# Four edits to a fused Fourier layer and two-layer MLP: a later negation, a third transform on 94 columns, operands moved to multiples of 512 bytes, two chunks interleaved

## The chip, the core and the metric

The kernel runs on one core of one Trainium2 chip. The metric is the device time in microseconds of one execution; lower is better. Times are compared as the median of several executions; the profile is one further execution.

## The reference

```python
# x: (2, 3008, 256); w_in: (256, 2048); w_out: (2048, 256); all float32
X = rfft(x, axis=1)
Yr = Xr @ w_r - Xi @ w_i + b_r
Yi = Xr @ w_i + Xi @ w_r + b_i
Y  = softshrink(Yr, 0.01) + 1j * softshrink(Yi, 0.01)
y  = irfft(Y, n=3008)                      # (2, 3008, 256)
x  = y.reshape(6016, 256)
h = x @ w_in1;  x = (max(h, 0) + alpha * min(h, 0)) @ w_out1
h = x @ w_in2;  g = where(h >= 1, h, where(h <= -1, 0, (h + 1)**2 / 4))
out = g @ w_out2
```

## The kernel before

**Fourier part.** The length 3008 is split as 47 x 64, so each transform is two small ones. `f1(g)` (16 groups, 8 per batch) is the first; its results go to DRAM (`store_a`) and come back in another layout (`load_a`). Then come 24 *items* (12 per batch): `f2` is the second transform of an item, and also splits its result into a high part `fh` (ScalarE) and a low part `fl` (VectorE's row `fl<-psf,fh`); `mix` multiplies by the two 256 x 256 weights with 24 matmuls; three VectorE operations add the bias and shrink (`t`, `clip`, `y`); `i1` is the first inverse transform, whose result `ve` goes to DRAM, one store for two items. `p3(g, c)` is the last inverse transform (16 groups, two column halves c, four float32 matmuls each, which the trace shows as eight records); it fills `y`, shown as `yt`. Item loop, step j: `f2` of item j+2, `mix` of j, `i1` of j-2; from j = 16 on also both halves of `p3(j-16)`, one evacuated by ScalarE, one by VectorE. The second batch's `p3` runs inside the MLP, one half per step.

**MLP.** The 6016 rows are 12 *chunks*, six per batch: 512, 512, 512, 512, 512, 448. For each layer l, chunk c and block f of 128 hidden features (16 blocks), `first(l, c, f)` does six matmuls into `psh` and the activation, whose result is split into `gh` and `gl`; `second` does six matmuls into two accumulators `pso`. A float32 product is made of three float32r matmuls, so lines 95, 96 and 97 are low weight by high data, high weight by low data, high by high; the streamed operand has 512 or 448 columns, and the operand loaded ahead of each is 128 x 128. `second` runs three steps behind `first`. `prep(l, c)` splits a chunk's input into `mxh` and `mxl`.

**Split early or late.** For most blocks of layer 0 VectorE makes `gh` at once. Where `late_split` holds (layer 1, and chunk 0 of layer 0) ScalarE makes it, in the step after.

**Weights.** They arrive as 64-bit words and are converted on chip. The generator `conversions` is advanced by `next(conv)`: its first call loads two blocks, then calls alternate between parts 2 and 0 (three operations each on ScalarE and VectorE) and parts 3 and 1 (four on VectorE, then a load of the block after next). Block f is complete after call 2f + 5. In the item loop there are 20 calls (none before j = 4), then one per step of chunk 0. A load is two DMAs of 256 KB from ScalarE's queue.

**Order.** Each engine executes its instructions in program order, and the program order is the order of the Python text. SyncE issues nearly all other DMAs, in text order too:

```python
    load_a(0, A_PARTS[3:])
    for g in range(8, 16):
        f1(g); store_a(g, 0)
    load_mn(1, n_t, c_i1)
    ...
    load_mn(2, m_t, c_f2)          # constants that f2 of items 8 to 11 multiplies by
    load_mn(2, n_t, c_i1)
    nc.sync.dma_start(nalpha, alpha)
    nc.sync.dma_start(g47, c_i2)
    load_a(1, A_PARTS)
```

`m_t[k]` serves `f2` of items 4k to 4k+3. `nalpha` holds alpha; it is negated on VectorE (line 288) and first used by the activation of `first(0, 0, 0)`.

**Addresses.** A tile takes its tag's place, and tags lie one behind another in each partition in the order of their first use. The tags p0 to p5, w0, w1 and m0 to m5 come ahead of `nalpha`, and each starts at a multiple of 512 bytes. `nalpha` takes 64 bytes of a partition, so all tags behind it (the other w and m, the c tags of `mxh` and `mxl`, `gh`, `gl`) start 64 bytes past such a multiple. Weight blocks lie in p, w and m tags (`w_tag`): in layer 0 five of 16 lie at a multiple (f = 10, 11, 13, 14, 15), in layer 1 nine (f = 0 to 5 and 9 to 11).

Of the kernel before, what the change touches and what calls it, by code (L numbers as in the profile page):

```python
# [17 lines left out]
R1, R2 = 47, 64  # L18
# [3 lines left out]
NF = DFF // 128  # L22
# [53 lines left out]
def spectral_mlp_kernel(ctx: ExitStack, tc: tile.TileContext, x, w_r, w_i, bias, c_f1, c_f2,  # L76
                        c_i1, c_i2, w_in1, w_out1, alpha, w_in2, w_out2, out):
    nc = tc.nc
    V, A, G, T = nc.vector, nc.scalar, nc.gpsimd, nc.tensor

    base = ctx.enter_context(tc.tile_pool(name="base", bufs=1))
    rot = ctx.enter_context(tc.tile_pool(name="rot", bufs=2))
    psum = ctx.enter_context(tc.tile_pool(name="psum", bufs=4, space=PSUM))
    dram = ctx.enter_context(tc.tile_pool(name="dram", bufs=1, space=DRAM))

    def split(src, hi, lo, hi_engine):

# [15 lines left out]
    def block(tag, shape, dtype, name):  # L103
        return base.tile(shape, dtype, tag=tag, name=name)
# [16 lines left out]
    def w_of(l, k, f, h, sl):  # L121
        return wt[l, f][:, h, 256 * k + sl * 128:256 * k + sl * 128 + 128]
# [70 lines left out]
    ps = psum.tile([128, 256], F32, tag="h", name="ps_warm")  # L193
# [58 lines left out]
    m_t = [block(f"m{k}", [128, 8, 128], F32, f"m{k}") for k in range(3)]  # L252
    n_t = [block(f"m{3 + k}", [128, 8, 128], F32, f"n{k}") for k in range(3)]
    wm32 = [rot.tile([128, 2, D], F32, tag="tb", name=f"wm32_{k}") for k in range(2)]
    nalpha = base.tile([128, NF], F32, name="nalpha")
    g47 = base.tile([96, 128], F32, name="g47")
    b_t = base.tile([128, 1, D], F32, name="b_t")
    for g in range(8):
# [26 lines left out]
    wm = [block(f"c{k}", [128, 2, 2, D], F32R, f"wm{k}") for k in range(2)]  # L285
    for k in range(2):
        split(wm32[k], wm[k][:, 0], wm[k][:, 1], A)
    V.tensor_scalar(nalpha, nalpha, -1.0, None, op0=ALU.mult)


    items = [(b, i) for b in range(B) for i in range(NK // 2)]
# [51 lines left out]
    for b in range(B):  # L343
        c0 = 0
# [3 lines left out]
    NMAX = max(CHUNKS)  # L348
    NC = len(chunks)
    xc, gt, po = {}, {}, {}  # L350

    def prep(l, c):
        b, c0, n = chunks[c]
        k = 2 * (c % 2)
        xh = block(f"c{k}", [128, 2, NMAX], F32R, f"mxh{l}_{c}")
        xl = block(f"c{k + 1}", [128, 2, NMAX], F32R, f"mxl{l}_{c}")
        split(y[b][:, :, c0:c0 + n], xh[:, :, :n], xl[:, :, :n], A)
        xc[l, c] = xh, xl

    vs, y = {}, [None] * B  # L360

    def load_v(g):
        b, j = divmod(g, 8)
        vs[g] = block(f"m{6 + g % 3}" if b == 0 else f"m{j}", [96, 4, D], F32, f"v{b}_{j}")
        nc.sync.dma_start(vs[g], v_dr[b][:, 4 * j:4 * j + 4, :])

    def p3(g, c, engine):
        b, j = divmod(g, 8)
        if y[b] is None:
            y[b] = block(f"a{b}", [128, 2, S], F32, f"yt{b}")  # L370
        ps = psum.tile([128, 4, 128], F32, tag="h", name=f"ps3_{b}_{j}_{c}")
# [3 lines left out]
        if engine is A:
            A.activation(dst, ps[:, :, 0:94], AF.Copy)
        else:
            V.tensor_copy(dst, ps[:, :, 0:94])


    def late_split(step):
        return step[0] == 1 or step[:2] == (0, 0)

    def split_late(step):
        if step is not None and late_split(step):
            gh, gl, ta = gt[step]
            split(ta, gh, gl, A)

    def first(l, c, f, before):
        n = chunks[c][2]  # L390
        xh, xl = xc[l, c]
        ps = psum.tile([128, NMAX], F32, tag="h", name=f"psh{l}_{c}_{f}")[:, :n]
        for d in range(2):
            mm3(ps, w_of(l, 0, f, 0, d), w_of(l, 0, f, 1, d), xh[:, d, :n], xl[:, d, :n], d == 0, d == 1)
        gh = rot.tile([128, NMAX], F32R, tag="gh", bufs=4, name=f"gh{l}_{c}_{f}")[:, :n]
        gl = rot.tile([128, NMAX], F32R, tag="gl", bufs=4, name=f"gl{l}_{c}_{f}")[:, :n]
        ta = rot.tile([128, NMAX], F32, tag="ta", name=f"ta{l}_{c}_{f}")[:, :n]
        tb = rot.tile([128, NMAX], F32, tag="tb", name=f"tb{l}_{c}_{f}")[:, :n]
        gt[l, c, f] = gh, gl, ta
        if l == 0:  # L400

            A.activation(ta, ps, AF.Relu, scale=-1.0)  # L402
# [33 lines left out]
    conv = conversions(0, list(range(NF)), V, V)  # L436
    n = len(items)
    P3_AT = 16
    for j in range(2):
        f2(*items[j])  # L440
    for j in range(n):
        if j + 2 < n:
            f2(*items[j + 2])
        mix(*items[j])
        if j >= 2:
            i1(*items[j - 2])
        if j == 13:
# [77 lines left out]
```

## Time and profile before

| | us |
|---|---|
| median of 3 runs (lowest, highest) | 1261.45 (1260.71, 1262.11) |
| profiled execution, its own time | 1261.51 |
| its span in the trace | 1259.7 |
| TensorE busy in the span | 1208.5 |
| VectorE / ScalarE busy | 926.3 / 588.7 |

The profiled execution's span is 1.8 us shorter than its own time; its time is within 0.1 us of the median, so differences in the trace can be read as differences in the median. TensorE matmuls overlap in the trace (a record is longer than the distance to the next), so the pace of matmuls is read from their starts.

### The profile page before, as it was taken

What the parts mean: (1) busy time and instruction counts of PE and PEld (TensorE: products, weight loads), DVE (VectorE), ACT (ScalarE), POOL (GpSimd) and SP (SyncE); (2) the same over time, 40 slices, a digit from 0 to 9 for tenths busy, and PEclk for the clock granted to TensorE, in tenths of its full rate; (3) what the DMA queues carried; (4) which work ended last, traced back from release to release, by engine and by line L of the source; (5) the groups of instructions that cost most, each with busy time, mean ns of one, the idle gap of its engine ahead of it and who ended that gap; (6) DMA issues with size and microseconds to landing.
All of it is one profiled execution on the core that took longest, in us unless ns stands there. A gap on an engine that the chain in (4) does not pass through costs nothing.

```text
span 1259.7 us, 15641 instructions
## 1 busy us (share of the span) xinstructions
PE 1208.5 (96%) x5862; PEld 1026.6 (81%) x5862; DVE 926.3 (74%) x1449; ACT 588.7 (47%) x1091; POOL 83.3 (7%) x64
## 2 busy tenths in 40 slices
PE   9179998999999999999999999999999999999998
PEld 6179996878888898888888878888888888888888
DVE  3047787957788999898677798777776777777765
ACT  3035546844555455544444544444444444444443
POOL 0000000000122322131000041000000000000000
PEclk9689998999999999999999999999999999999999
DMA  9943547101010101000000100000000000000000
GB/s 276 290 176 117 158 144 196 39 1 34 18 34 17 34 18 34 17 1 1 1 1 1 51 17 1 18 17 17 1 17 17 15 1 17 18 1 18 17 17 16
DMA packets 37180, 59.30 MB, mean 47 GB/s; under 512 B 3248, under 2 KB 25200, under 8 KB 37104
## 3 DMA queue, kind: packets, MB, share of 16 engines
q1 hardware_dynamic: 23536, 41.37, 10.5%
q10 hardware_dynamic: 13568, 16.93, 4.2%
q8 instruction: 46, 0.75, 0.2%
q14 instruction: 30, 0.25, 0.1%
HBM read 39.55 MB, written 18.74 MB: 46 GB/s over the span
## 4 chain that ended last, share of the span: by engine, by line
PE 90%; DVE 3%; DMA 3%; SPq 2%; ACT 1%; issue 1%; ACTq 0%; DVEq 0%
PE pso L96 13%; PE pso L95 13%; PE psh L95 13%; PE psh L96 13%; PE pso L97 13%; PE psh L97 13%; PE ps L373 2%; PE psm L318 2%; PE psm L320 2%; PE psm L319 2%; PE ps L243 2%; PE psf L298 1%; PE psi L333 1%; SPq L224 1%; DMA a_dr<-ae 1%; DVE gl L92 1%
## 5 line engine op out<-in xcount | busy, mean ns | idle before, releaser
L95 PE MATMUL pso<-gh,w 128*128 128x512 f32 (+1 forms) x768 | 298.6, 389 | 2.8 <-ACT gh L89 2.8
L95 PE MATMUL psh<-mxh,w 128*128 128x512 f32 (+1 forms) x768 | 297.6, 387 | 3.4 <-DVE w L162 2.2
L96 PE MATMUL pso<-gl,w 128*128 128x512 f32 (+1 forms) x768 | 298.3, 388 | 2.5 <-DVE gl L92 2.5
L96 PE MATMUL psh<-mxl,w 128*128 128x512 f32 (+1 forms) x768 | 297.5, 387 | 0.0
L97 PE MATMUL pso<-gh,w 128*128 128x512 f32 (+1 forms) x768 | 296.2, 386 | 0.0
L97 PE MATMUL psh<-mxh,w 128*128 128x512 f32 (+1 forms) x768 | 295.8, 385 | 0.0
L92 DVE TENSOR_TENSOR gl<-ta,gh 128x512 fp32r<-128x512 f32 (+1 forms) x384 | 277.1, 722 | 18.1 <-ACT gh L89 12.0
L410 ACT ACTIVATE ta<-psh 128x512 f32<-128x512 f32 (+1 forms) x192 | 113.1, 589 | 281.6 <-PE psh L97 248.8
L411 DVE SCALAR_TENSOR_TENSOR tb<-ta 128x512 f32<-128x512 f32 (+1 forms) x192 | 131.2, 683 | 137.7 <-ACT ta L410 136.7
L402 ACT ACTIVATE ta<-psh 128x512 f32<-128x512 f32 (+1 forms) x192 | 113.0, 589 | 248.9 <-PE psh L97 215.2
L405 DVE SCALAR_TENSOR_TENSOR ta<-ta,nalpha,tb 128x512 f32<-128x512 f32 (+1 forms) x192 | 166.4, 867 | 64.0 <-ACT tb L403 63.4
L95 PEld LDWEIGHTS psh<-mxh,w 128*128 128x128 f32 x768 | 144.4, 188 | 32.6 <-issue 2.6
L95 PEld LDWEIGHTS pso<-gh,w 128*128 128x128 f32 x768 | 144.5, 188 | 30.9 <-ACT gh L89 3.3
L96 PEld LDWEIGHTS pso<-gl,w 128*128 128x128 f32 x768 | 144.6, 188 | 30.7 <-DVE gl L92 4.7
L97 PEld LDWEIGHTS psh<-mxh,w 128*128 128x128 f32 x768 | 144.4, 188 | 27.9
L97 PEld LDWEIGHTS pso<-gh,w 128*128 128x128 f32 x768 | 144.4, 188 | 27.8
L96 PEld LDWEIGHTS psh<-mxl,w 128*128 128x128 f32 x768 | 144.5, 188 | 26.9
L89 ACT ACTIVATE gh<-ta 128x512 fp32r<-128x512 f32 (+1 forms) x208 | 128.4, 617 | 2.0 <-DVE ta L413 2.0
L413 DVE TENSOR_TENSOR ta<-psh,tb 128x512 f32<-128x512 f32 (+1 forms) x192 | 129.2, 673 | 0.0
L403 ACT ACTIVATE tb<-psh 128x512 f32<-128x512 f32 (+1 forms) x192 | 112.3, 585 | 0.0
L91 DVE CAST gh<-ta 128x512 fp32r<-128x512 f32 (+1 forms) x176 | 79.6, 452 | 18.1
L318 PE MATMUL psm<-wm,fl 128*128 128x256 f32 x192 | 56.3, 293 | 31.2 <-DVE fl L305 31.2
(57 smaller groups left out, 897.5 us busy)
## 6 DMA issues: line engine op xcount, KB each, us to landing
u<-in_w_in ACTq DMA_DIRECT2D x32, 256.0 KB, 2.7
u<-in_w_out ACTq DMA_DIRECT2D x32, 256.0 KB, 3.0
v_dr<-ve SPq DMA_DIRECT2D x12, 512.0 KB, 3.7
v<-v_dr SPq DMA_DIRECT2D x16, 384.0 KB, 6.1
x<-in_x SPq DMA_DIRECT2D x15, 384.0 KB, 8.0
out<-yt SPq DMA_DIRECT2D x20, 256.0 KB, 2.2
a<-a_dr SPq DMA_DIRECT2D x6, 768.0 KB, 6.8
a_dr<-ae SPq DMA_DIRECT2D x20, 192.0 KB, 6.9
```

Of the source, the lines that this page charges most:

```text
L89: A.activation(hi, src, AF.Copy)
L92: V.tensor_tensor(lo, src, hi.bitcast(F32), op=ALU.subtract)
L95: T.matmul(ps, wl, xh, start=start, stop=False)
L96: T.matmul(ps, wh, xl, start=False, stop=False)
L97: T.matmul(ps, wh, xh, start=False, stop=stop)
L318: T.matmul(o, xl[:, j, off:off + 128], wm[r][:, 0, c, :], start=c == r == 0, stop=False)
L402: A.activation(ta, ps, AF.Relu, scale=-1.0)
L403: A.activation(tb, ps, AF.Relu)
L405: V.scalar_tensor_tensor(ta, ta, nalpha[:, f:f + 1], tb, op0=ALU.mult, op1=ALU.add)
L410: A.activation(ta, ps, AF.Relu, bias=0.5, scale=0.5)
L411: V.scalar_tensor_tensor(tb, ta, 1.0, ta, op0=ALU.min, op1=ALU.mult)
L413: V.tensor_tensor(ta, ps, tb, op=ALU.max)
```

## The change

Four edits. (1) The negation of `nalpha` moves from ahead of the item loop into it, at j = 20. (2) `p3` multiplies 94 columns instead of 128 of which 94 were used, and ScalarE evacuates both halves. (3) `nalpha` takes 512 bytes of a partition, so that all tags behind it start at multiples of 512 bytes; for chunks of 448, `mxh`, `mxl`, `gh` and `gl` are used from the 16th column on (`window`), 64 bytes past a multiple. (4) Chunks 0 and 1 of layer 0 go through the blocks together, chunk 1 four blocks behind: blocks 0 to 3 of chunk 0, then 4 of chunk 0, 0 of chunk 1, 5 of chunk 0, 1 of chunk 1, and so on. With it: both chunks split late; `prep(0, 1)` comes at step 2 and `prep(0, 2)` at step 26; the second batch's `p3` starts at step 8 instead of 4; the item loop has one call of the conversions in each step from j = 3 to 21 (19 calls), the MLP's first 32 steps two in every three.

```diff
-    nalpha = base.tile([128, NF], F32, name="nalpha")
+    nalpha = base.tile([128, 128], F32, name="nalpha")[:, 0:NF]
...
-    V.tensor_scalar(nalpha, nalpha, -1.0, None, op0=ALU.mult)
...
+    def window(n):
+        return slice(0, n) if n == NMAX else slice(16, 16 + n)
...
-        split(y[b][:, :, c0:c0 + n], xh[:, :, :n], xl[:, :, :n], A)
+        split(y[b][:, :, c0:c0 + n], xh, xl, A)
...
-    def p3(g, c, engine):
+    def p3(g, c):
-        ps = psum.tile([128, 4, 128], F32, tag="h", name=f"ps3_{b}_{j}_{c}")
+        ps = psum.tile([128, 4, 2 * R1], F32, tag="h", name=f"ps3_{b}_{j}_{c}")
-            T.matmul(ps[:, i, :], vs[g][:, i, c * 128:(c + 1) * 128], g47, start=True, stop=True)
+            T.matmul(ps[:, i, :], vs[g][:, i, c * 128:(c + 1) * 128], g47[:, 0:2 * R1], start=True, stop=True)
+        A.activation(dst, ps, AF.Copy)
...
-        return step[0] == 1 or step[:2] == (0, 0)
+        return step[0] == 1 or step[1] < 2
...
+        if j == 20:
+            V.tensor_scalar(nalpha, nalpha, -1.0, None, op0=ALU.mult)
         if j == n - 2:
             prep(0, 0)
-        for _ in range((j >= 3 and j % 3 != 0) if j < P3_AT else 1 + j % 2):
-            next(conv, None)
+        if 3 <= j < n - 2:
+            next(conv)
...
-    first(0, 0, 1, (0, 0, 0))
-    DEPTH = 3
-    seq = [(l, c, f) for l in range(2) for c in range(NC) for f in range(NF)]
+    DEPTH, LEAD = 3, 4
+    pair = sorted([(0, c, f) for c in range(2) for f in range(NF)], key=lambda s: (s[2] + LEAD * s[1], s[1]))
+    seq = pair + [(l, c, f) for l in range(2) for c in range(NC) for f in range(NF) if (l, c) not in ((0, 0), (0, 1))]
...
-            if 4 <= i < 20:
-                p3(8 + (i - 4) // 2, i % 2, A)
-            if ((l, c) == (0, 0) and f < 15 or (l, c) in ((0, NC - 1), (1, 0)) and f % 2 == 0
+            if i == 2:
+                prep(0, 1)
+            if 8 <= i < 24:
+                p3(8 + (i - 8) // 2, i % 2)
+            if (i < 2 * NF and i % 3 != 0 or (l, c) in ((0, NC - 1), (1, 0)) and f % 2 == 0
                     or l == 0 and c >= 2 and f % 4 == 0):
                 next(conv, None)
```

Three places in the order of instructions. The first is VectorE's queue after the last evacuations of `f1`: the weights' low parts (`wm`), then what stands ahead of the first item's `fl`. Before:

```order
L92 TENSOR_TENSOR wm_321<-wm_0_105,wm_321 128x512
L92 TENSOR_TENSOR wm_322<-wm_1_106,wm_322 128x512
L288 TENSOR_SCALAR nalpha<-nalpha 128x16
L305 TENSOR_TENSOR fl_0_334<-psf_0_328,fh_0_333 128x4x128
L305 TENSOR_TENSOR fl_1_345<-psf_1_339,fh_1_344 128x4x128
```

Of the change:

```order
L92 TENSOR_TENSOR wm_321<-wm_0_105,wm_321 128x512
L92 TENSOR_TENSOR wm_322<-wm_1_106,wm_322 128x512
L304 TENSOR_TENSOR fl_0_333<-psf_0_327,fh_0_332 128x4x128
L304 TENSOR_TENSOR fl_1_344<-psf_1_338,fh_1_343 128x4x128
L304 TENSOR_TENSOR fl_2_355<-psf_2_349,fh_2_354 128x4x128
```

The row on `nalpha` is gone from here; nothing else moved. The second place is ScalarE's queue at steps j = 3 and 4 of the item loop, where `ve` is `i1`'s evacuation, `u` is a raw weight block and `cm` its first conversion. Before:

```order
L336 ACTIVATE ve_0_479<-psi_1_523 128x512
L303 ACTIVATE fh_6_533<-psf_6_528 128x4x128
L304 ACTIVATE fh_6_533<-psf_6_528 128x4x64
L306 ACTIVATE fl_6_534<-fl_6_534 128x4x64
L336 ACTIVATE ve_2_573<-psi_2_570 128x512
L127 DMA u_0_575<-in_w_in 128x2x256
L129 DMA u_0_575<-in_w_out 128x512
L127 DMA u_1_578<-in_w_in 128x2x256
L129 DMA u_1_578<-in_w_out 128x512
```

Of the change:

```order
L335 ACTIVATE ve_0_478<-psi_1_522 128x512
L127 DMA u_0_527<-in_w_in 128x2x256
L129 DMA u_0_527<-in_w_out 128x512
L127 DMA u_1_530<-in_w_in 128x2x256
L129 DMA u_1_530<-in_w_out 128x512
L302 ACTIVATE fh_6_538<-psf_6_533 128x4x128
L303 ACTIVATE fh_6_538<-psf_6_533 128x4x64
L305 ACTIVATE fl_6_539<-fl_6_539 128x4x64
L335 ACTIVATE ve_2_578<-psi_2_575 128x512
L140 ACTIVATE cm_0_580<-u_0_527 128x512
```

The first weight loads stand one item earlier, and the conversion that waits for them follows at the next item. The third place is VectorE's queue at the start of the MLP, where `cm`, `cp`, `w` and `u` are conversions, `ta` is the activation of a block, and `gl_0_0` is what `second(0, 0, 0)` needs. Before:

```order
L326 TENSOR_TENSOR y_1_11_1679<-t_11_1678,clip_11_1677 128x512
L378 COPY yt_1202<-ps_0_7_1_1694 128x376
L161 TENSOR_TENSOR cm_7_1579<-cm_7_1579,w_7_1643 128x512
L162 TENSOR_TENSOR w_7_1643<-cm_7_1579,cp_7_1580 128x512
L168 TENSOR_SCALAR cm_8_1647<-cm_8_1647 128x512
L153 SCALAR_TENSOR_TENSOR cm_8_1647<-cm_8_1647,cp_8_1648 128x512
L158 TENSOR_SCALAR cp_8_1648<-cm_8_1647 128x512
L159 TENSOR_TENSOR cp_8_1648<-cp_8_1648,u_8_1513 128x512
L142 TENSOR_SCALAR cp_9_1712<-u_9_1588 128x512
L405 SCALAR_TENSOR_TENSOR ta_0_0_1730<-ta_0_0_1730,nalpha,tb_0_0_1731 128x512
L92 TENSOR_TENSOR gl_0_0_1729<-ta_0_0_1730,gh_0_0_1728 128x512
```

Of the change:

```order
L325 TENSOR_TENSOR y_1_11_1686<-t_11_1685,clip_11_1684 128x512
L405 SCALAR_TENSOR_TENSOR ta_0_0_1721<-ta_0_0_1721,nalpha,tb_0_0_1722 128x512
L92 TENSOR_TENSOR gl_0_0_1720<-ta_0_0_1721,gh_0_0_1719 128x512
L405 SCALAR_TENSOR_TENSOR ta_0_1_1756<-ta_0_1_1756,nalpha,tb_0_1_1757 128x512
L158 TENSOR_SCALAR cp_8_1537<-cm_8_1536 128x512
L159 TENSOR_TENSOR cp_8_1537<-cp_8_1537,u_8_1329 128x512
L142 TENSOR_SCALAR cp_9_1768<-u_9_1467 128x512
L92 TENSOR_TENSOR gl_0_1_1755<-ta_0_1_1756,gh_0_1_1754 128x512
L405 SCALAR_TENSOR_TENSOR ta_0_2_1781<-ta_0_2_1781,nalpha,tb_0_2_1782 128x512
L92 TENSOR_TENSOR mxl_1_1789<-yt_1240,mxh_1_1788 128x1024
```

Between the last item's `y` and the first block's `ta`, eight rows are gone; `mxl_1`, the second chunk's input, now stands ahead of the third block's `gl`.

## Rows read from the trace of the kernel before

**Rows 1.** The page's part 1: busy us, share of the span, instructions.

```profile
PE 1208.5 (96%) x5862; PEld 1026.6 (81%) x5862; DVE 926.3 (74%) x1449; ACT 588.7 (47%) x1091; POOL 83.3 (7%) x64
```

**Rows 2.** VectorE's timeline, 26 to 90 us: start, duration, operation, [idle before, releaser].

```profile
70.27 0.17 DVE L288 TENSOR_SCALAR nalpha<-nalpha 128x16 f32<-128x16 f32 x1 [33.79 <-DMA nalpha<-in_alpha]
```

**Rows 3.** TensorE's timeline, 38 to 98 us, from the first waiting `mix` on.

```profile
38.81 1.13 PE L298 MATMUL psf<-m,a 128*128 128x128 f32 x8 [1.98 <-DMA m<-in_c_f]
71.09 0.58 PE L318 MATMUL psm<-wm,fl 128*128 128x256 f32 x1 [31.15 <-DVE fl L305]
...
75.69 1.05 PE L298 MATMUL psf<-m,a 128*128 128x128 f32 x8
...
79.41 1.05 PE L298 MATMUL psf<-m,a 128*128 128x128 f32 x8
...
97.44 0.39 PE L298 MATMUL psf<-m,a 128*128 128x128 f32 x2
```

**Rows 4.** SyncE's load of `m_t[2]`: issue time (62 to 75 us) and time to landing.

```profile
L227 SPq DMA_DIRECT2D m<-in_c_f x1: 550/550/550, 63.4 to 63.4; - x1
...
DMA to landing us min/median/max: 5.3/5.3/5.3
```

**Rows 5.** One stretch, all engines: busy us and instructions, granted clock, DMA share, GB/s.

```profile
61.00:66.00 5.00, 0.00 (x0) 0.00 (x0) 0.00 (x0) 0.00 (x0) 0.00 (x0) 0.50 1.03 318
```

**Rows 6.** TensorE's timeline at the start of the MLP, 202 to 254 us.

```profile
202.16 0.50 PE L95 MATMUL pso<-gh,w 128*128 128x512 f32 x1 [2.84 <-ACT gh L89]
...
208.24 2.07 PE L373 MATMUL ps<-g,v 96*128 96x128 f32 x8 [2.59 <-DMA v<-v_dr]
...
209.97 0.77 PE L95 MATMUL pso<-gh,w 128*128 128x512 f32 x1
...
211.82 0.63 PE L96 MATMUL pso<-gl,w 128*128 128x512 f32 x1
212.25 0.63 PE L97 MATMUL pso<-gh,w 128*128 128x512 f32 x1
...
247.74 0.47 PE L95 MATMUL psh<-mxh,w 128*128 128x512 f32 x1 [1.16 <-ACT yt L376]
...
253.86 0.47 PE L95 MATMUL psh<-mxh,w 128*128 128x512 f32 x1 [2.23 <-DVE w L162]
```

**Rows 7.** ScalarE's timeline ahead of the first activation of the MLP.

```profile
196.92 0.63 ACT L156 ACTIVATE w<-cm 128x512 fp32r<-128x512 f32 x1 [4.82 <-DVE cm L153]
...
199.06 0.58 ACT L402 ACTIVATE ta<-psh 128x512 f32<-128x512 f32 x1
```

**Rows 8.** TensorE's timeline: four pairs of starts in the MLP.

```profile
573.45 0.39 PE L95 MATMUL psh<-mxh,w 128*128 128x512 f32 x1
...
589.77 0.39 PE L95 MATMUL psh<-mxh,w 128*128 128x512 f32 x1
...
832.05 0.39 PE L95 MATMUL psh<-mxh,w 128*128 128x512 f32 x1
...
840.29 0.39 PE L95 MATMUL psh<-mxh,w 128*128 128x512 f32 x1
...
446.19 0.37 PE L95 MATMUL psh<-mxh,w 128*128 128x448 f32 x1
...
458.59 0.37 PE L95 MATMUL psh<-mxh,w 128*128 128x448 f32 x1
...
962.81 0.36 PE L95 MATMUL psh<-mxh,w 128*128 128x448 f32 x1
...
970.01 0.36 PE L95 MATMUL psh<-mxh,w 128*128 128x448 f32 x1
```

**Rows 9.** Groups of weight loads by shape: count, busy us, mean ns, idle before.

```profile
L373 PEld LDWEIGHTS ps<-g,v 96*128 96x128 f32 x256 | 33.1, 196 | 4.6 <-DMA v<-v_dr 3.0
...
L243 PEld LDWEIGHTS ps<-x,c 96*96 96x96 f32 x128 | 21.4, 169 | 9.3 <-issue 1.7 <-DMA x<-in_x 0.5
```

**Rows 10.** The chain that ended last, in order of time: start, us, what.

```profile
184.23 1.79 PE ps L373 x16
```

More of the change, by code (lines that the diff above doesn't have):

```diff
@@ L354, in prep @@
         k = 2 * (c % 2)
-        xh = block(f"c{k}", [128, 2, NMAX], F32R, f"mxh{l}_{c}")
-        xl = block(f"c{k + 1}", [128, 2, NMAX], F32R, f"mxl{l}_{c}")
-        split(y[b][:, :, c0:c0 + n], xh[:, :, :n], xl[:, :, :n], A)
+        xh = block(f"c{k}", [128, 2, NMAX], F32R, f"mxh{l}_{c}")[:, :, window(n)]
+        xl = block(f"c{k + 1}", [128, 2, NMAX], F32R, f"mxl{l}_{c}")[:, :, window(n)]
+        split(y[b][:, :, c0:c0 + n], xh, xl, A)
         xc[l, c] = xh, xl
@@ L370, in p3 @@
             y[b] = block(f"a{b}", [128, 2, S], F32, f"yt{b}")
-        ps = psum.tile([128, 4, 128], F32, tag="h", name=f"ps3_{b}_{j}_{c}")
+        ps = psum.tile([128, 4, 2 * R1], F32, tag="h", name=f"ps3_{b}_{j}_{c}")
         for i in range(4):
-            T.matmul(ps[:, i, :], vs[g][:, i, c * 128:(c + 1) * 128], g47, start=True, stop=True)
+            T.matmul(ps[:, i, :], vs[g][:, i, c * 128:(c + 1) * 128], g47[:, 0:2 * R1], start=True, stop=True)
         dst = y[b][:, c, 376 * j:376 * j + 376].rearrange("p (i n) -> p i n", i=4)
[L375 to L378, printed above, removed]
+        A.activation(dst, ps, AF.Copy)
     def late_split(step):
-        return step[0] == 1 or step[:2] == (0, 0)
+        return step[0] == 1 or step[1] < 2
     def split_late(step):
@@ L393, in first @@
         for d in range(2):
-            mm3(ps, w_of(l, 0, f, 0, d), w_of(l, 0, f, 1, d), xh[:, d, :n], xl[:, d, :n], d == 0, d == 1)
-        gh = rot.tile([128, NMAX], F32R, tag="gh", bufs=4, name=f"gh{l}_{c}_{f}")[:, :n]
-        gl = rot.tile([128, NMAX], F32R, tag="gl", bufs=4, name=f"gl{l}_{c}_{f}")[:, :n]
+            mm3(ps, w_of(l, 0, f, 0, d), w_of(l, 0, f, 1, d), xh[:, d, :], xl[:, d, :], d == 0, d == 1)
+        gh = rot.tile([128, NMAX], F32R, tag="gh", bufs=4, name=f"gh{l}_{c}_{f}")[:, window(n)]
+        gl = rot.tile([128, NMAX], F32R, tag="gl", bufs=4, name=f"gl{l}_{c}_{f}")[:, window(n)]
         ta = rot.tile([128, NMAX], F32, tag="ta", name=f"ta{l}_{c}_{f}")[:, :n]
@@ L451, in spectral_mlp_kernel @@
             g = j - P3_AT
-            p3(g, 0, A)
-            p3(g, 1, V)
+            p3(g, 0)
+            p3(g, 1)
             if g + 3 < 8:
                 load_v(g + 3)
+        if j == 20:
+            V.tensor_scalar(nalpha, nalpha, -1.0, None, op0=ALU.mult)
         if j == n - 2:
             prep(0, 0)
-        for _ in range((j >= 3 and j % 3 != 0) if j < P3_AT else 1 + j % 2):
-            next(conv, None)
+        if 3 <= j < n - 2:
+            next(conv)
     i1(*items[n - 2])
@@ L479, in spectral_mlp_kernel @@
                 conv = conversions(1, list(range(12, 16)), V, G)
-            if i >= 2:
+            if i >= 1:
                 first(l, c, f, seq[i - 1])
-            if 4 <= i < 20:
-                p3(8 + (i - 4) // 2, i % 2, A)
-            if ((l, c) == (0, 0) and f < 15 or (l, c) in ((0, NC - 1), (1, 0)) and f % 2 == 0
+            if i == 2:
[3 more added lines that the diff above has]
+            if (i < 2 * NF and i % 3 != 0 or (l, c) in ((0, NC - 1), (1, 0)) and f % 2 == 0
                     or l == 0 and c >= 2 and f % 4 == 0):
                 next(conv, None)
-            if f == NF // 2:
+            if (l, c, f) == (0, 0, NF - 1):
+                prep(0, 2)
+            elif f == NF // 2 and (l, c) not in ((0, 0), (0, 1)):
                 nxt = (l, c + 1) if c + 1 < NC else (l + 1, 0)
```

## The prediction

> **What bounds the kernel now.** I read the page's busy times first. TensorE is busy for 1208.5 of 1259.7 us [rows 1]; no other engine comes near. So a gain must come either from the 51 us in which TensorE waits or from the pace of its matmuls. VectorE's and ScalarE's busy time matters only where TensorE waits for them.
>
> Then I looked for the waits in TensorE's timeline. One is larger than all others together: 31.15 us ahead of the first `mix`, at 71.09 us, for VectorE's `fl` [rows 3]. VectorE's timeline shows why: it stood idle for 33.79 us until alpha had landed, and negated it in 0.17 us at 70.27 [rows 2]; `fl` stands right behind. Sixteen numbers per partition, which no activation needs before 199 us [rows 7], held the queue. The second place is the start of the MLP, where the timeline shows waits of 2.84 and 2.59 us, then steps of 0.43 us at half the clock, then waits of 1.16 and 2.23 us [rows 6]. The rest of the MLP hardly waits, so there I read the pace.
>
> Pace. Two starts with a known number of matmuls between them give it [rows 8]. 72 matmuls on 512 columns between 573.45 and 589.77 us (layer 0, blocks whose weights lie 64 bytes past a multiple of 512, as the streamed operand does) take 16.32 us: 226.7 ns each. 36 between 832.05 and 840.29 us (layer 1, weights at a multiple, stream 64 past) take 8.24: 228.9 ns. On 448 columns, 60 between 446.19 and 458.59 us (both 64 past): 206.7 ns; 36 between 962.81 and 970.01 us (weights at a multiple, stream 64 past): 200.0 ns. At half the clock a step on 512 columns takes 0.43 us [rows 6], half of which, about 213, is what the full clock should need. So 13 to 20 ns of each step are something else, and it depends on where the operands lie. The four paces are near 213.3 or 186.7 plus two or three times 6.67 ns.
>
> **Edit 1, the negation.** Nothing on VectorE waits for alpha any more at 36 us, so `fl` and the first `mix` follow the second transform of item 2, which starts at 38.81 us [rows 3]. What is late next is a transfer. A step of the item loop is one `f2` and one `mix`: 79.41 - 75.69 = 3.72 us [rows 3]; with `i1` it is 4.5, since the five steps from item 3's `f2` (75.69) to item 8's (97.44) took 21.75 us, one without and four with `i1`. From 38.81 us the first step and those five reach item 8's `f2` at 38.8 + 3.7 + 21.75 = 64.3 us, but its constants are issued at 63.4 and land 5.3 us later, at 68.7 [rows 4]. SyncE's issues do not depend on the items, so that transfer comes no earlier. It can come later: the first weight loads now start at j = 3, near 56 us, into queues that are full (share 1.03, 318 GB/s [rows 5]). Two blocks are 1 MB, 3.3 us at that rate; with the third block 4.9. I take 4: landing at 72.7, item 8's `f2` at 72.8 instead of 97.44, a gain of 24.6. The wait of some 8 us lets the clock fall; in the trace the `mix` after such a wait took 4.60 us (71.09 to 75.69), while a warm step with `f2` takes 3.72, of which `f2` is 0.8: a loss of 1.7 that is not saved but moved. **Gain 23 us.** Bounds: 27 with no contention; about 12 if conversions and loads hold the items for another ten, since a call of the conversions stands in every item now and VectorE's work per item comes near TensorE's 4.5 us.
>
> **Edit 4, the start of the MLP.** Before, conversions stand between the last item's `y` and the first activation: ScalarE waits 4.82 us for VectorE's `cm`, and starts the first block's `ta` at 199.06 us [rows 7], five us after its matmuls. That makes the 2.84 us wait. The calls of the last two item steps are gone from there, so `gl_0_0` should be ready when the four blocks' `first` are done. The 2.59 us are `p3` waiting for `v`; four steps of 2.7 us later the data are there. Without these two waits the clock should not fall: eight `p3` records took 1.73 us (208.24 to 209.97) instead of half of 1.79 [rows 10], and the eleven matmuls behind them 0.43 instead of 0.227, together 3.0 us. The 1.16 and 2.23 us are block 13's buffer and block 15's weights; chunk 0 now uses a block every second step, call 35 comes at step 23, and block 15 is used at step 26. Sum 2.84 + 2.59 + 3.0 + 1.16 + 2.23 = 11.8. Against it: `prep(0, 1)` now stands ahead of the third block's `gl`, and until `p3` starts at step 8 both engines have nearly as much to do per step as TensorE. I leave one wait of the size seen, 2.8. **Gain 9 us**; bounds 3 (the waits return in another form) and 12. Chunk 1's late split moves work from VectorE to ScalarE under busy matmuls, at nothing; if that cover were gone it would be one `gh` per step, and it would show as a wait of `pso`.
>
> **Edit 3, addresses.** For 448 columns the new pair (weights at a multiple, stream 64 past) stands in the trace at 200.0 ns. Weights lie 64 past in 11 of 16 blocks in layer 0 and 7 in layer 1; with two such chunks per layer and 12 matmuls per block that is 2 x 18 x 12 = 432 matmuls x 6.7 = 2.9 us. For 512 columns the new pair (both at a multiple) is not in the trace. I take it to depend on the distance between the two addresses alone, as for two streams that meet in the same memory; then it is 226.7, as where both are 64 past, and the 14 of 32 blocks at 228.9 gain 2.2 ns: 10 chunks x 14 x 12 = 1680 x 2.2 = 3.7 us. **Gain 6.5 us.** Bounds: no excess, 213.3 ns, would gain 3840 x 13.3 = 51 us more; one more piece of 6.67 ns, the third that 448 columns show, would lose 3840 x 6.67 = 26. I choose the middle since the only rows with equal addresses show it.
>
> The Trainium skill ("TensorE: Matmul & The Clock Gate", Back-to-back issue gap) gives a warm matmul N / 2.4 + 2.5 ns, 215.8 for 512 columns. No stretch here reaches that, and by it the aligned pairs would save some 42 us more than I count.
>
> **Edit 2, 94 columns.** Sixteen records take 1.79 us [rows 10], 112 ns each. If streaming set this, 94 / 128 of it would save 30 ns on 256 records, 7.6 us. But each needs a load of 128 columns of `v`, and loads of 96 and 128 columns take 169 and 196 ns [rows 9]: 27 for 32 columns, so some 108 of the 112 ns are the load's own streaming, which the edit leaves alone. **Gain 0.3 us** (0 to 7.6). That ScalarE evacuates both halves is hidden by 6 us of matmuls per item.
>
> The same page (LDWEIGHTS) says that a load's time follows its columns, at P / 1.2 ns, 107 for 128, whatever the matmul behind it streams. By that rule edit 2 is worth nothing, and the rows agree.
>
> **Sum.** 23 + 9 + 6.5 + 0.3 = 38.8 us. Profiled execution 1261.5, median 1261.45: 1222.7, rounded to **1222 us**.
>
> **Rivals.** A: the transfers hold the items longer, the lower bound of edit 1: 1222 + 11 = 1233. For it: full queues [rows 5]; against it: little is left to land after 78 us. B: the MLP's start waits again (bound 3): 1228. C: equal addresses at a multiple lose half the excess, one piece: 1222 - 26 = 1196. D: they lose all of it: 1222 - 51 = 1171; the rule above would give 1180. For both speaks that the excess vanishes at half the clock; against, that no full-clock pair of the four shows less than two pieces. E: one piece more: 1248. F, the other side: two pieces more, 240 ns, cost 51 us and give 1273, slower than before; it decides from 237 ns per step on (39 us over 3840 matmuls, 10 ns). Against: no pair shows more than three pieces. G: the shorter `p3` and the equal addresses do nothing (512 columns stay at their mean of 227.6): 1226, inside the forecast's range.
>
> **Numbers.** Forecast with G 0.60 (its own range 1214 to 1229), A 0.08, B 0.05, C 0.09, D 0.09, E 0.06, F 0.03. The range takes in A, B and C: 1193 to 1235. A measurement of this kernel tells a change of 0.2%, 2.5 us, from none. Faster 0.96, within 0.2% 0.01, slower 0.03.
>
> **What would show it.** First `mix` near 40 us; item 8's `f2` waiting for `m` until 69 to 74 us; no steps of 0.43 us near the MLP's start, no wait there over 3 us; 226.7 ns on 512 columns and 200.0 on 448 in all blocks; `p3` still near 110 ns. The prediction is wrong if the items wait for weights or conversions after 75 us, or if the aligned pace is another: each ns on 512 columns is 3.8 us.

## The result, and the profile after

The changed kernel takes 1225.96 us (median of 4 runs, 1225.43 to 1229.38) against 1261.78 us (4 runs, 1260.71 to 1262.82) beside it: the ratio is 0.972, 95% interval 0.970 to 0.974, 35.8 us less. The prediction was 1222 us, a gain of 38.8; direction and range held, and the gain is 3 us short. The profiled execution took 1225.43 us, its span is 1223.6 us.

The page of the changed kernel, part 1 (columns as in [rows 1]):

```profile
PE 1204.8 (98%) x5862; PEld 1028.9 (84%) x5862; DVE 913.1 (75%) x1425; ACT 598.8 (49%) x1115; POOL 82.9 (7%) x64
```

TensorE is busy 3.7 us less than in [rows 1], but the span is 36.1 us shorter: most of the gain is waiting that is gone. TensorE's timeline of the changed kernel shows where (it answers to [rows 3]):

```profile
38.86 0.56 PE L317 MATMUL psm<-wm,fl 128*128 128x256 f32 x1
...
71.78 2.07 PE L297 MATMUL psf<-m,a 128*128 128x128 f32 x8 [6.83 <-DMA m<-in_c_f]
...
78.40 1.02 PE L332 MATMUL psi<-y,n 128*128 128x256 f32 x4
...
90.53 0.39 PE L317 MATMUL psm<-wm,fl 128*128 128x256 f32 x1 [0.94 <-DVE t L323]
...
99.14 1.05 PE L297 MATMUL psf<-m,a 128*128 128x128 f32 x8
...
102.91 1.03 PE L332 MATMUL psi<-y,n 128*128 128x256 f32 x4
```

The first `mix` starts at 38.86 us, not 71.09. Item 8's `f2` starts at 71.78 us, not 97.44 [rows 3], after 6.83 us of waiting for `m_t[2]`. That load is now issued at 65.71 us and lands 6.0 us later (63.4 and 5.3 before [rows 4]). The later issue goes with the first weight loads: they start at 55.72 us instead of 93.17, and in the waits of SyncE's queue from 28 to 82 us one wait of 4.2 us for such a load stands ahead of it, which the kernel before does not have. The wait costs a second time: from this `f2` to the `i1` behind its `mix` pass 6.62 us (71.78 to 78.40), for a later item 3.77 us (99.14 to 102.91), so 2.85 us go at the lower clock, which the windows show as a granted clock of 0.50 (1.2 GHz) from 71.78 to 77.70 us.

Behind the short wait of 0.94 us at 90.53 us lies a longer one on another engine. ScalarE's timeline of the changed kernel:

```profile
86.17 0.60 ACT L335 ACTIVATE ve<-psi 128x512 f32<-128x512 f32 x1 [10.17 <-DMA v_dr<-ve]
```

`ve` of item 4 takes the buffer of items 0 and 1, whose store to DRAM was not done. ScalarE is held for 10.17 us, with the next `fh` queued behind. TensorE loses only the 0.94 us and some 0.4 us behind them (10.61 us from the item at 88.53 us to the second one behind it at 99.14, where two steps of 4.64 us make 9.28), since the items ahead had been held up themselves and kept it busy until 89.6 us.

At the start of the MLP, TensorE's timeline of the changed kernel (it answers to [rows 6]; this row is the only one with a wait that the view prints between 172 and 274 us):

```profile
186.87 0.50 PE L96 MATMUL pso<-gl,w 128*128 128x512 f32 x1 [1.34 <-DVE gl L92]
```

The waits of 2.84, 2.59, 1.16 and 2.23 us are gone, and so are the steps of 0.43 us at half the clock: from 172.5 to 274 us the granted clock is 1.00. The 1.34 us for `gl` is new.

The pace, from starts in TensorE's timeline of the changed kernel (it answers to [rows 8]):

```profile
573.76 0.39 PE L95 MATMUL psh<-mxh,w 128*128 128x512 f32 x1
...
590.08 0.39 PE L95 MATMUL psh<-mxh,w 128*128 128x512 f32 x1
...
833.88 0.39 PE L95 MATMUL psh<-mxh,w 128*128 128x512 f32 x1
...
842.04 0.39 PE L95 MATMUL psh<-mxh,w 128*128 128x512 f32 x1
...
958.71 0.36 PE L95 MATMUL pso<-gh,w 128*128 128x448 f32 x1
959.31 0.36 PE L95 MATMUL pso<-gh,w 128*128 128x448 f32 x1
```

72 matmuls on 512 columns in 16.32 us and 36 in 8.16 us: 226.7 ns in both layers. Three on 448 columns in 0.60 us: 200 ns.

Four places in the traces of the kernels with and without each edit (us from the start of the span):

| | `f2` of item 8 | first `psh` | first `psh` of chunk 2 | end of span |
|---|---|---|---|---|
| before | 97.44 | 192.01 | 304.96 | 1259.7 |
| changed | 71.78 | 172.51 | 274.00 | 1223.6 |
| negation early again | 97.96 | 194.50 | 295.99 | 1245.6 |
| pair undone | 73.45 | 172.30 | 284.69 | 1234.6 |
| addresses undone | 74.70 | 171.88 | 273.38 | 1228.1 |

### The profile page after: what moved, and what is told of

It reads as the page before. It is cut to its first block, busy times and chain, and to the rows that moved or that the text cites. A ratio compares the mean times of both kernels' runs of the same rounds, so it can differ in the third digit from the quotient of the medians.

```text
span 1223.6 us, 15634 instructions
## 1 busy us (share of the span) xinstructions
PE 1204.8 (98%) x5862; PEld 1028.9 (84%) x5862; DVE 913.1 (75%) x1425; ACT 598.8 (49%) x1115; POOL 82.9 (7%) x64
## 4 chain that ended last, share of the span: by engine, by line
PE 91%; DMA 4%; DVE 3%; ACT 1%; issue 1%; SPq 0%; ACTq 0%; DVEq 0%
PE pso L96 14%; PE pso L97 13%; PE pso L95 13%; PE psh L97 13%; PE psh L96 13%; PE psh L95 13%; PE ps L376 2%; PE psm L317 2%; PE psm L319 2%; PE psm L318 1%; PE psf L297 1%; PE psi L332 1%; DMA v_dr<-ve 1%; DMA m<-in_c_f 1%; DVE gl L92 1%; DMA x<-in_x 1%
## 5 line engine op out<-in xcount | busy, mean ns | idle before, releaser
L89 ACT ACTIVATE gh<-ta 128x512 fp32r<-128x512 f32 (+1 forms) x224 | 138.7, 619 | 2.0 <-DVE ta L413 2.0
L91 DVE CAST gh<-ta 128x512 fp32r<-128x512 f32 (+1 forms) x160 | 72.7, 454 | 16.8 <-DVE ta L405 0.5
```

## The experiments

**The negation put back.**

```diff
+    V.tensor_scalar(nalpha, nalpha, -1.0, None, op0=ALU.mult)
...
-        if j == 20:
-            V.tensor_scalar(nalpha, nalpha, -1.0, None, op0=ALU.mult)
```

> The change with the negation of alpha back ahead of the item loop. Theory (the negation held VectorE's queue): the 31 us wait ahead of the first mix returns, the transfer of m_t[2] is no longer waited for, and the MLP starts 19 to 20 us later; 1245 us. Rival (most of the items' gain comes from the earlier and steadier conversions, and the negation only shifts a wait): 1233 or less.

Measured: 1246.52 us (4 runs), ratio to before 0.988, interval 0.986 to 0.990; 20.6 us over the changed kernel. VectorE's row and then TensorE's in its timelines:

```profile
70.45 0.17 DVE L288 TENSOR_SCALAR nalpha<-nalpha 128x16 f32<-128x16 f32 x1 [33.94 <-DMA nalpha<-in_alpha]
```
```profile
71.28 0.58 PE L318 MATMUL psm<-wm,fl 128*128 128x256 f32 x1 [28.86 <-DVE fl L305]
```

The old wait is back with the one row, and `m_t[2]`, issued at 63.4 us again, is no longer waited for. The theory stands. In the two traces the difference is 22.0 us, not 20.6, at the first `psh` as at the end: the execution profiled here was the slowest of its four, that of the changed kernel the fastest.

**The pair undone.** The order of blocks, the calls of the conversions, the early split of chunk 1 and the places of `prep` and `p3` as before; the other three edits kept.

```diff
-    pair = sorted([(0, c, f) for c in range(2) for f in range(NF)], key=lambda s: (s[2] + LEAD * s[1], s[1]))
-    seq = pair + [(l, c, f) for l in range(2) for c in range(NC) for f in range(NF) if (l, c) not in ((0, 0), (0, 1))]
+    seq = [(l, c, f) for l in range(2) for c in range(NC) for f in range(NF)]
...
```

> The change without edit 4: chunk 0 alone, then chunk 1, with the old places of the conversions, of prep and of the second batch's p3. Theory (edit 4 removes the waits at the MLP's start and the fall of the clock behind them): waits of 2 to 3 us near psh of blocks 3 and 4 and steps of 0.43 us return there; about 11 us more than the change, 1237 us. Rival (the waits went because the items are no longer held up, not because of the order): within 3 us of the change, 1226 to 1229.

Measured: 1235.94 us (ratio 0.979, interval 0.977 to 0.981), 10.0 us over the changed kernel. The four longest of its waits of TensorE from 172 to 286 us (what waits, for what: us in total, times, longest):

```profile
PE pso L95 <- ACT gh L89: 2.3, 1, 2.3
PE ps L376 <- DMA v<-v_dr: 2.2, 1, 2.2
PE psh L95 <- DVE w L162: 2.2, 1, 2.2
PE psh L95 <- ACT yt L378: 1.3, 1, 1.3
```

The four waits of [rows 6] return, each within 0.6 us of its size before, and so do the cold steps: from 189.44 to 194.28 us the granted clock is 0.50. The rival is out.

**The addresses undone.**

```diff
-    nalpha = base.tile([128, 128], F32, name="nalpha")[:, 0:NF]
+    nalpha = base.tile([128, NF], F32, name="nalpha")
...
-        return slice(0, n) if n == NMAX else slice(16, 16 + n)
+        return slice(0, n)
```

> The change without edit 3: nalpha takes 64 bytes, all tags behind it start 64 bytes past a multiple of 512, 448 columns start where the tile does. Theory (addresses give back 6 us in the MLP and cost 2 to 3 us in mix, whose matmuls on 256 columns went from 113 to 118 ns to 120): 3 us more than the change, about 1229 us; mix at 113 or 118 ns again, 228.9 ns and 206.7 ns again in the MLP. Rival (the pace of mix has another cause, so undoing the addresses costs all 6): 1232 us, mix still at 120 ns.

Measured: 1230.27 us (ratio 0.975, interval 0.973 to 0.977), 4.3 us over the changed kernel. From chunk 2 on the addresses are worth 5.1 us (954.7 against 949.6 us to the end of the span, from the table). But in the items the other sign shows. Two pairs of starts, each pair within one `mix`, in TensorE's timeline, first of the changed kernel, then of this one:

```profile
109.42 0.28 PE L318 MATMUL psm<-wm,fh 128*128 128x256 f32 x1
...
110.98 0.28 PE L319 MATMUL psm<-wm,fh 128*128 128x256 f32 x1
```
```profile
109.69 0.28 PE L318 MATMUL psm<-wm,fh 128*128 128x256 f32 x1
...
110.82 0.28 PE L319 MATMUL psm<-wm,fh 128*128 128x256 f32 x1
```

13 steps in 1.56 us are 120 ns each, 10 steps in 1.13 us are 113 ns. The edit that helps the MLP made `mix` slower. Over the 16 items behind the wait for `m_t[2]`, the mean step is 119.6 ns with the edit and 115.3 without, as before the change: 384 x 4.3 = 1.65 us. The trace with the edit undone reaches the first `psh` only 0.6 us earlier, though, since `m_t[2]` was issued at 70.0 us there and item 8 began 2.9 us later. So 5.1 less 0.6 is the 4.5 us between the two spans.

**The pace of matmuls alone.** This kernel holds only matmuls, 48 or 72 (24 of plain float32) for each pair of addresses, behind a constant's load; nothing of the layer is computed.

```diff
+    for n in (512, 448):
+        for m in (0, 16, 32, 48, 64, 80, 96, 112):   # stream's offset, in 4-byte elements
+            run(n, m, (0,))
+    for m, k in ((16, 16), (32, 32), (64, 64), (0, 16), (0, 64), (4, 0), (8, 0)):
+        run(512, m, (k,))
+    for m, k in ((16, 16), (0, 16)):
+        run(448, m, (k,))
+    for m in (0, 16, 32, 48, 64, 80, 96, 112):
+        run(256, m, (0, 64), count=72)
+    for n, cols in ((128, 128), (94, 128), (32, 128), (128, 64), (94, 64), (94, 96)):
+        plain(n, cols)
```

> Only streams of matmuls of one kind each, 48 or 72 in a row, with a new weight load ahead of each; the layer's work is left out and the output is zeros. The number behind m is the streamed operand's start and the one behind w the weights' start, in bytes past a multiple of 512; the first number is the columns streamed (t: float32r, f: float32). Theory 1 (the distance of the two addresses decides): 512 columns at equal starts (000/000, 064/064, 128/128, 256/256) all 226.7 ns; 064/000 about 229; 448 columns 000/000 and 064/064 206.7, 064/000 200.0. Theory 2 (the place decides, an operand at a multiple of 512 is cheaper by itself): 064/064 on 512 columns slower than 000/000, 000/064 slower than 000/000 whatever the distance, and 448 columns best at 000/000. On 256 columns with weights at 000 and 256 in turn: near 120 ns with the stream at 000, 113 to 118 at 064. Float32 rows (c is the number of weight columns): if loading the weights sets the pace, 128, 94 and 32 streamed columns all take about 112 ns with 128 weight columns, and 94 columns take about 81 with 64 weight columns; if streaming sets it, 94 columns take about 82 and 32 about 30 with 128 weight columns.

Measured, in its TensorE timeline (a name holds t, columns, m and the stream's offset in bytes, w and the weights', z between alternating ones; f, the plain columns, c, the loaded columns):

```profile
24.89 11.04 PE L103 MATMUL t512m000w000x<-mv,w 128*128 128x512 f32 x48
35.77 11.17 PE L103 MATMUL t512m064w000x<-mv,w 128*128 128x512 f32 x48
46.77 11.32 PE L103 MATMUL t512m128w000x<-mv,w 128*128 128x512 f32 x48
57.93 11.36 PE L103 MATMUL t512m192w000x<-mv,w 128*128 128x512 f32 x48
69.13 11.06 PE L103 MATMUL t512m256w000x<-mv,w 128*128 128x512 f32 x48
80.03 11.17 PE L103 MATMUL t512m320w000x<-mv,w 128*128 128x512 f32 x48
...
113.39 9.88 PE L103 MATMUL t448m000w000x<-mv,w 128*128 128x448 f32 x48
123.11 9.77 PE L103 MATMUL t448m064w000x<-mv,w 128*128 128x448 f32 x48
...
152.21 10.08 PE L103 MATMUL t448m256w000x<-mv,w 128*128 128x448 f32 x48
162.13 9.76 PE L103 MATMUL t448m320w000x<-mv,w 128*128 128x448 f32 x48
...
287.82 8.80 PE L103 MATMUL t256m000w000z256x<-mv,w 128*128 128x256 f32 x72
296.45 8.64 PE L103 MATMUL t256m064w000z256x<-mv,w 128*128 128x256 f32 x72
...
313.48 8.35 PE L103 MATMUL t256m192w000z256x<-mv,w 128*128 128x256 f32 x72
321.67 8.78 PE L103 MATMUL t256m256w000z256x<-mv,w 128*128 128x256 f32 x72
...
355.50 5.52 PE L111 MATMUL f128c128x<-raw,vf 96*128 96x128 f32 x48
360.86 5.50 PE L111 MATMUL f094c128x<-raw,vf 96*128 96x94 f32 x48
366.19 8.73 PE L111 MATMUL f032c128x<-raw,vf 96*128 96x32 f32 x48
```

Differences of starts over the count (the distance is the stream's offset less the weights'): on 512 columns 226.7 ns at distance 0, 229.2 at 64 bytes, 232.5 at 128, 233.3 at 192, 227.1 at 256 again; 16 and 32 bytes already cost some 232 and 233. Equal offsets of 64, 128 and 256 bytes in both operands gave 227 to 228, and weights 64 bytes past the stream (distance 192) 233.3. That is theory 1. On 448 columns it missed: 202.5 ns at distance 0 and 202.7 with both at 64, where 206.7 was expected, and 206.7 at 256, so there 0 and 256 are not the same; 200.2 at 64 was as expected. On 256 columns the order turns round: 119.9 ns at 0, 117.9 at 64, 113.8 at 192.

Plain float32, whose matmul shows two records: 111.7 ns a record on 128 columns, 111.0 on 94. On 32 columns the first records, still at a granted clock of 1.00, are 112 ns apart too; then the clock falls (see the last section). Behind a load of 64 columns, 94 columns take 82.7 ns (48 records from 383.43 to 387.40 us). So with 128 columns to load the load sets the pace.

**The third transform on 128 columns again.**

```diff
-        ps = psum.tile([128, 4, 2 * R1], F32, tag="h", name=f"ps3_{b}_{j}_{c}")
+        ps = psum.tile([128, 4, 128], F32, tag="h", name=f"ps3_{b}_{j}_{c}")
...
-            T.matmul(ps[:, i, :], vs[g][:, i, c * 128:(c + 1) * 128], g47[:, 0:2 * R1], start=True, stop=True)
+            T.matmul(ps[:, i, :], vs[g][:, i, c * 128:(c + 1) * 128], g47, start=True, stop=True)
...
-        A.activation(dst, ps, AF.Copy)
+        A.activation(dst, ps[:, :, 0:94], AF.Copy)
```

> The changed kernel with 128 columns in the third transform again. Theory (the load of the weights of 128 columns sets the 112 ns of one of these matmuls, so 94 columns gave nothing): 1226.0 us, within 1 us, and the start of one matmul to the next stays at 112 ns. Rival (the matmul's own length counts): 256 matmuls that took 26.9 us in sum grow as 128 to 94, to 36.6 us, +9.7 us, 1235.7 us.

Measured: 1225.53 us (5 runs), ratio to before 0.972, interval 0.970 to 0.973: no difference from the changed kernel. The chain that ended last holds the same sixteen records in both, first with 94 columns, then with 128:

```profile
133.52 1.76 PE ps L376 x16
```
```profile
134.29 1.79 PE ps L376 x16
```

110 and 112 ns a record: the shorter stream gives 2 ns, 0.5 us over 256 records.

**The tiles of `fh` and `fl` moved by 64 bytes,** so that in `mix` the weights start 64 bytes past a multiple of 256 and the stream `wm` at one: distance 192 as counted above. Before the change it was the other way round, the stream 64 past and `fh` and `fl` at a multiple: distance 64. "As it was" in the expectation holds for the size alone.

```diff
-        xh = piece([128, 4, 192], F32R, f"fh{b}_{i}")
-        xl = piece([128, 4, 192], F32R, f"fl{b}_{i}")
+        xh = piece([128, 784], F32R, f"fh{b}_{i}")[:, 16:784].rearrange("p (j n) -> p j n", j=4)
+        xl = piece([128, 784], F32R, f"fl{b}_{i}")[:, 16:784].rearrange("p (j n) -> p j n", j=4)
```

> The changed kernel with the tiles of fh and fl moved by 64 bytes, so that in mix the distance between the streamed operand (wm) and the weights (fh, fl) is 192 or 448 bytes, as it was in items 3 to 16 before the change; nothing else moves. Theory (the distance sets the pace, and the change itself cost mix 6.7 ns per matmul): 120.0 ns falls to 113.3 ns in all 576 matmuls of mix. The eight items ahead of the wait for m_t[2] only wait longer for it, so 16 items of 24 matmuls count: 384 x 6.7 ns = 2.6 us, 1223.4 us in all. First rival (the pace of mix is set by where the weights lie alone, or by neither): 120 ns and 1226.0 us. Second rival (all 576 count): 1222.1 us.

Measured: 1225.39 us (1223.13 to 1226.45), ratio 0.971, interval 0.970 to 0.973: within the measurement of the changed kernel. The pace did change. Two items in its timeline:

```profile
109.50 0.28 PE L317 MATMUL psm<-wm,fl 128*128 128x256 f32 x1
...
111.62 0.28 PE L317 MATMUL psm<-wm,fl 128*128 128x256 f32 x1
...
114.09 0.28 PE L317 MATMUL psm<-wm,fl 128*128 128x256 f32 x1
...
116.13 0.28 PE L317 MATMUL psm<-wm,fl 128*128 128x256 f32 x1
```

18 steps in 2.12 us (117.8 ns) in one item and 2.04 us (113.3) in the next, at the same distance; the mean over the last 16 items is 115.3 ns. So the addresses matter, but the expected 113.3 ns holds only in some of the items, and the distance alone does not tell in which: before the change, at distance 64, 14 items ran at 113.4 ns and 9 at 117.7 to 118.0. The wait for `m_t[2]` in front of them ended 1.5 us later than in the changed kernel's profile (73.28), which took up most of the 1.65 us.

**The 448 columns without the offset.**

```diff
-        return slice(0, n) if n == NMAX else slice(16, 16 + n)
+        return slice(0, n)
```

> The changed kernel without the offset of 64 bytes for chunks of 448 columns: streamed operand and weights then both stand at multiples of 256 bytes for them, distance 0. Theory (equal places cost the matmuls of 448 columns time, as in the kernel with the third edit undone, where they ran at 206.5 ns against 200 to 201 in the changed one): 768 matmuls of 448 columns x 6 ns = +4.6 us, 1230.6 us. Rival (as in the run of matmuls alone, 202 ns at distance 0): 768 x 1.5 ns = +1.2 us, 1227.2 us. The matmuls of 512 columns stay at 226.7 ns under both.

Measured: 1228.09 us (1226.81 to 1229.16), ratio 0.974, interval 0.972 to 0.975. Starts of chunks 5 and 6 of layer 0, first of the changed kernel, then of this one:

```profile
404.56 0.37 PE L95 MATMUL psh<-mxh,w 128*128 128x448 f32 x1
...
443.55 0.39 PE L95 MATMUL psh<-mxh,w 128*128 128x512 f32 x1
```
```profile
404.61 0.36 PE L95 MATMUL psh<-mxh,w 128*128 128x448 f32 x1
...
444.00 0.40 PE L95 MATMUL psh<-mxh,w 128*128 128x512 f32 x1
```

38.99 against 39.39 us, four such chunks: 1.6 us. The rival is right. At distance 0 with both operands at a multiple of 512 bytes a matmul on 448 columns takes some 202 ns, not the 206.7 of [rows 8], where both stood 64 bytes past. What made those slower is open: the run of matmuls alone has 202.7 ns for both at 64 too.

**What is late next: the load of `m_t[2]` moved ahead, the stores of `v` in another queue, and both.**

```diff
     load_mn(1, m_t, c_f2)
     load_a(0, A_PARTS[3:])
+    load_mn(2, m_t, c_f2)
...
-    load_mn(2, m_t, c_f2)
...
-            nc.sync.dma_start(dst[:, 2 * i - 2:2 * i + 2, :], ve[b])
+            queue = A if (b, i) in ((0, 1), (0, 3)) else nc.sync
+            queue.dma_start(dst[:, 2 * i - 2:2 * i + 2, :], ve[b])
```

The load alone (the first two places of the diff):

> The changed kernel with the load of m_t[2] moved ahead in SP's queue, from behind all stores of the second half of the first transform to right behind the last load of the first a. Theory (TensorE waited for m_t[2] alone at 65 to 72 us, 6.8 us, and lost about 2.8 us more at the lower clock behind it): the 6.8 us and the cold start go, but the store of v behind ScalarE's ve, which waited 10.2 us at 86 us, is no earlier, since it stands in the same queue behind the loads; TensorE then waits there for most of what was won, and the gain is 2 to 6 us: 1220 to 1224 us. Rival (m_t[2] was the last thing late): -9.6 us, 1216 us. Second rival (the loads share one rate, and the load moved ahead delays the last pieces of a): 1226 us or more.

The stores alone (the last place):

> The changed kernel with the first two stores of v of batch 0 issued from ScalarE's queue, and the load of m_t[2] where the change has it. Theory (TensorE is held by two things in turn, the load of m_t[2] and then the store behind ve): the wait for m_t[2] of about 7 us and its cold start of 2.8 us stay, and only the 0.94 us and some 0.3 us behind ve's wait go: 1224.7 us. With the load alone moved, 9.1 us of waiting for ve came in place of the wait for m_t[2]; with both, 12.4 us went; so the two alone should give about -1.2 and +1.6, and only together -12.4. Rival (the store alone holds the items): 1214 to 1217 us.

Both:

> As the kernel with the load of m_t[2] moved ahead, and the first two stores of v of batch 0 are issued from ScalarE's queue, not SP's, so that they do not stand behind the loads of the second half. Theory (the wait for m_t[2], and behind it the wait of ve for its buffer, hold TensorE): both go, -8 to -10 us, 1216 to 1218 us, and no idle time of TensorE over 1 us is left between 45 and 160 us. Rival (the transfers share one rate, so the store lands as late from either queue): 1220 to 1224 us, as with the load alone.

Measured: load alone 1227.53 us (ratio 0.973, interval 0.972 to 0.975), stores alone 1225.85 us (0.972, 0.970 to 0.975), both 1213.59 us (1212.78 to 1214.61; 0.962, 0.961 to 0.964). With the load alone, ScalarE's `ve` and then TensorE behind it:

```profile
89.38 0.60 ACT L335 ACTIVATE ve<-psi 128x512 f32<-128x512 f32 x1 [16.90 <-DMA v_dr<-ve]
```
```profile
90.03 2.07 PE L332 MATMUL psi<-y,n 128*128 128x256 f32 x4 [9.14 <-ACT ve L335]
```

SyncE issues that store only at 78.06 us, behind its loads for the second batch. So the load alone missed its 1220 to 1224 us, since the wait for `ve` took all that was won. Its time is the second rival's, but no wait of TensorE for `a` stands between 34 and 180 us. With the stores alone, `m_t[2]` is waited for as in the changed kernel:

```profile
74.22 2.07 PE L297 MATMUL psf<-m,a 128*128 128x128 f32 x8 [7.11 <-DMA m<-in_c_f]
```

With both, TensorE's waits from 34 to 175 us come down to:

```profile
PE psf L297 <- DMA m<-in_c_f: 2.5, 2, 1.7
PE pso L96 <- DVE gl L92: 1.3, 1, 1.3
```

The first of these is over at 45.2 us; from 45 to 160 us the granted clock is 1.00 and TensorE is busy 114.79 of 115 us. Neither edit alone gives anything (1.6 us more and 0.1 us less than the changed kernel), both give 12.4 us: two waits lay one behind the other, and either alone was enough to hold the items.

**Both, with the tiles moved as well.**

> The load of m_t[2] early, the first two stores of v from ScalarE's queue, and the tiles of fh and fl moved by 64 bytes. Theory: no wait of TensorE takes up what mix gains any more, so all 576 matmuls of mix count, at the 115.3 ns that they had on average in the kernel with moved tiles against 119.7 ns: -2.5 us beside the 1213.6 us of the kernel with early load and stores alone, 1211.1 us. Rival (DMA paces the first items, so that the gain is eaten by a longer wait there): 1213.6 us.

Measured: 1214.53 us (1211.99 to 1215.47; ratio 0.962, interval 0.961 to 0.964), not to be told from 1213.59. In its profile the mean step of `mix` behind the first item is 115.8 ns, but its first `mix` started at 39.92 us instead of 37.53, since the first constants came later, and at 99.75 us TensorE waited 1.42 us for `t`, behind a `ve` that waited 3.52 us for its store. The 2.5 us expected of the pace are the size of that scatter, so what the tiles are worth in time was not shown. The kernel with load and stores alone beats both kernels of the comparison.

## Why the prediction was right

| term | predicted | measured by undoing it |
|---|---|---|
| edit 1, negation | 23 (12 to 27) | 20.6 |
| edit 4, pair | 9 (3 to 12) | 10.0 |
| edit 3, addresses | 6.5 (-26 to 51) | 4.3 |
| edit 2, 94 columns | 0.3 (0 to 7.6) | -0.4, none |
| sum | 38.8 | 34.5; all at once 35.8 |

**Edit 1.** The mechanism was as predicted: `m_t[2]` is late next, and item 8's `f2` came at 71.78 us where 72.8 was said. The term was mis-sized in what is given back behind it. "A loss of 1.7" for the cold start measured 2.85 us: the row it came from, 4.60 us, was that of a `mix` that began cold, without the `f2` ahead of it at the lower clock. Some 1.3 us went at the wait for `t` at 90 us, behind the store of `v`, which no term named. Against the kernel with the negation put back, whose `mix` has the same pace, item 8 won 26.2 us; less these two that leaves 22.0, which is what the first `psh` shows. Against the kernel before, 25.7 us were won and 19.5 are left: there the slower `mix` of edit 3 takes 1.65 us more, and 0.3 us is not assigned.

The 4 us taken for contention were 3.0 (71.7 us to land, not 68.7), and by another way than the sum has it: 2.3 of them are a later issue, since SyncE's own queue waited for the weight loads, and 0.7 a longer transfer.

**Edit 4.** Right: the four waits and the cold steps went, and came back when it was undone. In the traces all of it lies between the first `psh` and chunk 2: 101.5 us in the changed kernel, 112.4 with the edit undone. The 2.8 us left for a wait "of the size seen" was too much; one wait of 1.34 us stands there.

**Edit 3.** "I take it to depend on the distance between the two addresses alone" is right for 512 columns: 226.7 to 227.7 ns for equal addresses wherever they lie, so no piece was lost or gained, and rivals C to F are out. For 448 columns 200 ns held in both layers, but the statement did not: distance 0 shows 206.7 ns in [rows 8], but some 202 in the kernel without the offset and in the run of matmuls alone. The step that failed is the count of what the edit reaches: only the MLP's matmuls were counted. The 576 of `mix` got new distances too, and slower ones: 119.6 ns for 115.3, 1.65 us behind item 8. That and less from the MLP (5.1 us from chunk 2 on) brought 6.5 down to the measured 4.3.

The Trainium skill ("TensorE: Matmul & The Clock Gate", Back-to-back issue gap) gives 215.8 ns for 512 columns at N / 2.4 + 2.5, as the gap of a warm matmul taken by itself. No pair of addresses tried here shows it; the measured 226.7 to 233.3 ns decide, for matmuls that each have a load of 128 columns.

**Edit 2.** Right. 94 and 128 columns behind a load of 128 columns run at 110 to 112 ns.

The Trainium skill ("TensorE: Matmul & The Clock Gate", LDWEIGHTS) puts a load of 128 columns at P / 1.2, 107 ns; the measured 110 to 112 ns lie close to it.

**The other rivals.** A and B (transfers hold the items longer, the MLP's start waits again) happened in small: 1.3 and 1.34 us, not 11 and 6. G was half right, since edit 2 gave nothing; the 512 columns did reach 226.7 ns. That the measured 1226 us is G's own number is chance: what is missing went in edit 1 and in `mix`.

## What to carry to other kernels

When a wait goes, walk the queue that was behind it to the next late thing and the one after; here two waits one behind the other gave nothing when either was removed (1.6 us more, 0.1 us less) and 12.4 us when both were. When a tile moves, list all matmuls that read behind it, not only those that it was moved for. A shorter stream behind a full load of weights bought nothing here: compare the two before shortening one.

## What the runs showed of the hardware

The pace of float32r matmuls, each with its own load, follows the distance of the two operands in a partition, on 512 and 256 columns with a period of 256 bytes (512 columns: 226.7, 229.2, 232.5, 233.3 ns at 0, 64, 128, 192, then 227.1 at 256); on 448 columns 0 and 256 differ (202.5 and 206.7 ns). What is best turns with the length: on 256 columns distance 0 is the slowest (119.9 ns) and 192 the fastest (113.8). At one distance, `mix` with the moved tiles ran at 113.3 ns in some items and 117.8 in others, mostly in turn; why is open.

TensorE's granted clock fell in the run of matmuls alone while the engine was without a gap: during plain float32 matmuls on 32 columns behind loads of 128 columns, in its windows (columns: stretch, length, busy us of PE, PEld, DVE, ACT, POOL, granted clock, DMA share, GB/s):

```profile
360.00:366.00 6.00, 6.00 (x57) 6.00 (x56) 0.00 (x0) 0.00 (x0) 0.00 (x0) 1.00 0.01 3
...
370.00:374.80 4.80, 4.80 (x24) 4.79 (x23) 0.00 (x0) 0.00 (x0) 0.00 (x0) 0.50 0.00 0
```

The first stretch, all but its first 0.86 us on 94 columns, has a granted clock of 1.00 (2.4 GHz), the second, on 32 columns, 0.50 (1.2 GHz). No other run repeats this.
